# A decode step of attention and a gated MLP on one core: w_o loaded in two transfers instead of four, V's last block and w_up in plain runs, and one matmul moved

## The chip, the cores and the metric

One core of a Trainium2 chip runs the whole kernel. The time is device microseconds of one execution; a kernel's time is the median over several executions. One execution of each kernel is also recorded by the profiler. That gives the page, and behind it a trace with every instruction, every DMA packet and every semaphore event. All times inside the execution are counted from its first instruction.

## The reference

One token (x, 512 values) goes through a pre-norm attention block over a key and value cache of 65536 positions, with 32 query heads on 8 key/value heads of 128 dimensions, and then through a gated MLP of width 1792. All data are bf16.

```python
def _A_ref(x, k_cache, v_cache, wq, wo):        # x [1,1,512], wq [512,4096], wo [4096,512]
    q = (x @ wq).reshape(B, Sq, 32, 128).transpose(0, 2, 1, 3)
    k = jnp.repeat(k_cache, 4, axis=1)          # [1, 8, 65536, 128] -> 32 heads
    v = jnp.repeat(v_cache, 4, axis=1)
    scores = jnp.einsum("bhqd,bhkd->bhqk", q, k) * (128 ** -0.5)
    o = jnp.einsum("bhqk,bhkd->bhqd", _softmax(scores, axis=-1), v)
    return o.transpose(0, 2, 1, 3).reshape(B, Sq, 32 * 128) @ wo

def _B_ref(x, w_gate, w_up, w_down):            # [512,1792] twice, [1792,512]
    return (_sigmoid(x @ w_gate) * (x @ w_up)) @ w_down

h  = x + _A_ref(_layernorm(x), A_k_cache, A_v_cache, A_wq, A_wo)
h2 = h + _B_ref(_layernorm(h), B_w_gate, B_w_up, B_w_down)
```

The caches are 134 MB each. With the weights, the kernel reads 282.33 MB.

## The kernel before

**Blocks.** Each head's 65536 positions are cut into 4 blocks of 16384 (`NR` = 4), so there are 32 K blocks and 32 V blocks, K0 to K31 and V0 to V31, each of 4 MB. Partition p holds 128 consecutive positions of a block, which is one run of 32 KB in the cache. A ring of 4 slots of 32 KB per partition (`ring`) takes wq, all K and V blocks, and at the end the MLP's weights.

**Loads.** All of these loads are issued by SyncE (SP) on one queue, in the order of the list `order` (L289 to L293): wq, K0 to K3, then K and V in turns, then V28 to V31, w_gate, w_up, w_down. Each waits until its slot is free: for a K block that DVE has transposed it (`F{b}`), for a V block that PE has used it (`PV{b}`). SP issues in order, so a load that waits holds back those behind it. Directly after V28 come the loads of w_o (L347 to L352), into `ktw`, the buffer of the transposed K, when the last head's scores are done (`G7`). w_o is loaded in four pieces, `wo0` to `wo3`, of 16, 8, 4 and 4 heads (`WO`, L211). Partition p gets n consecutive rows for a piece of n heads, so the runs are 16, 8, 4 and 4 KB.

Three loads are split so that work can start on their first part. V31 (L339 to L343) is split at 3/4 into `V31.0` and `V31.1`. The block is seen as two halves of 16 KB per partition, and each transfer takes its share of both halves: two runs of 12 KB, then two of 4 KB. w_up is split into three of its four row groups and the fourth (`W_SPLIT`, L314), and w_down into 7, 5 and 2 of its 14 (`WD_SPLIT`, L212).

**Heads.** For each K block DVE transposes 8 chunks into `ktw` (L500), and PE makes the scores (L419, `ktw`). After 4 blocks there is a maximum over the head, the exponentials on ACT (L544) and a transpose on DVE (L554). One head later PE multiplies by V (L419, `ring,PT_sb`; 32 matmuls a block, four steps of 8), while the next head's K comes in. A step of V takes its rows from the first half of the block and the same place of the second half (`pv_regs`, L570; a step forward adds `CH`, L707); the K chunks are in the matching order (L495). PE's program is a loop; the parts that run only sometimes stand behind it and are branched to (`away`, L658). `head_out` (L587) normalizes a head's output and puts it into `O2`, 4 columns of 128 rows for the 4 query heads.

**The last heads.** w_o's rows are spread as n consecutive rows per partition, while `O2` holds a head's 128 dimensions on 128 partitions. `regroup(i)` (L601) brings the outputs of a piece into w_o's layout: DVE spreads the n columns over 128 columns with a mask (`blk_of`, L604), one matmul against a 0/1 matrix (`row_of`, L608) regroups them, and DVE copies the result to `O3` (L610). `project7` (L621) does this for the first three pieces, which hold the 28 heads 0 to 27, and then adds up 28 rows on PE (L627, L637, L645) into the row `yr`, to which DVE adds x (L647). It stands on PE between the work on V28 and on V29 (L763). SP issues `V31.0` when PE is done with V29, whose slot it takes. Before V31's work PE turns `yr` into columns (L649, `columns`); this part is branched to.

**The tail.** After V31: `head_out` for the last head, `regroup(3)` for its 4 query heads, 16 matmuls (L617), layer norm (L381 to L396), 16 matmuls with w_gate and 16 with w_up (L797). Between these stands the residual matmul (L803), which puts h into the PSUM bank of the final sum; it has to be there before w_down's matmuls add to that bank. Then tanh on ACT, the product (L809), a transpose (L812), 56 matmuls with w_down (L817), which wait for each of its three pieces, a copy and the output. Everything here depends on the step before.

**Setup.** DVE makes constants while wq is loaded, among them `row_of` and `blk_of` for n = 16, 8 and 4 (L369 to L373).

Of the kernel before, what the change touches and what calls it, by code (L numbers as in the profile page):

```python
# [6 lines left out]
bf16 = mybir.dt.bfloat16  # L7
fp32 = mybir.dt.float32
i32 = mybir.dt.int32
AF = mybir.ActivationFunctionType  # L10
ALU = mybir.AluOpType
# [184 lines left out]
def bass_sequential_preLN__gqa_block_cached__glu_gated_glu__decode_kernel(  # L196
# [11 lines left out]
    CH = TC * DH  # L208
    NF = FF // 128

    WO = ((0, 16), (16, 8), (24, 4), (28, 4))  # L211
    WD_SPLIT = [(0, 7), (7, 12), (12, 14)]  # L212
    FG = FF // 4

    with ExitStack() as es:
        def sb(name, shape, dt):
            return es.enter_context(nc.sbuf_tensor(name, shape, dt))
# [46 lines left out]

        W0 = NKT * CH
        O3 = sb("O3", [128, NQ], bf16)
        Lw = [sb(f"Lw{i}", [128, 128], bf16) for i in range(len(WO))]
        row_of = {n: sb(f"row_of{n}", [128, n], bf16) for n in (16, 8, 4)}
        blk_of = {n: sb(f"blk_of{n}", [128, 128 // n], bf16) for n in (16, 8, 4)}
        head_of = sb("head_of", [128, 4], fp32)  # L270
        assert 32 * D <= NKT * CH + WH
        KTW_ROW = NKT * CH + WH
# [3 lines left out]
        def ps(bank, c0, c1, p0=0, p1=128):  # L276
            return PS[p0:p1, bank * 512 + c0: bank * 512 + c1]
# [33 lines left out]

        dma("act", lambda e: e.dma_start(x_row[:, :], A_x[0]), "x", name="x")
        V_SPLIT = [(0, 3), (3, 4)]
        W_SPLIT = {"wg": [(0, 4)], "wu": [(0, 3), (3, 4)]}  # L314
        W_AT = {"wg": 0, "wu": 4 * FF}
        for ld in order:
            k, b = ld
            s = slot_of[ld]
            dst = slot_ap(s)
            deps = [freed(prev[ld])]  # L320
            if k == "wq":
                dma("sp", lambda e, d=dst: e.dma_start(d.rearrange("p (k n) -> p k n", k=4),
                    A_wq.rearrange("(p k) n -> p k n", p=128)), f"r{s}", deps, "wq")
            elif k in ("wg", "wu"):
                w = B_w_gate if k == "wg" else B_w_up
                dst, src = dst[:, W_AT[k]:W_AT[k] + 4 * FF], w.rearrange("(p k) n -> p (k n)", p=128)
                for i, (k0, k1) in enumerate(W_SPLIT[k]):
                    dma("sp", lambda e, d=dst, w=src, a=k0 * FF, z=k1 * FF: e.dma_start(d[:, a:z], w[:, a:z]),
                        f"{k}{i}", deps if i == 0 else (), f"{k}.{i}")
            elif k == "wd":  # L330
                src = B_w_down.rearrange("(p r) n -> p r n", p=128)
                for i, (r0, r1) in enumerate(WD_SPLIT):
                    dma("sp", lambda e, d2=dst[:, r0 * D:r1 * D].rearrange("p (r n) -> p r n", n=D), sr=src[:, r0:r1, :]:
                        e.dma_start(d2, sr), f"wd{i}", deps if i == 0 else (), f"wd{i}")
            else:
                h, r = b // NR, b % NR
                cache = A_k_cache if k == "K" else A_v_cache
                src = cache[0, h, r * BLK:(r + 1) * BLK, :].rearrange("(p t) d -> p (t d)", t=T)
                if ld == ("V", NB - 1):  # L339
                    for i, (c0, c1) in enumerate(V_SPLIT):  # L340
                        d2, s2 = (ap.rearrange("p (h c) -> p h c", h=2)[:, :, c0 * CH:c1 * CH] for ap in (dst, src))
                        dma("sp", lambda e, d2=d2, s2=s2: e.dma_start(d2, s2),
                            "v0" if i else "vl", deps if i == 0 else (), f"V{b}.{i}")  # L343
                else:
                    dma("sp", lambda e, d=dst, sr=src: e.dma_start(d, sr), f"v{s}" if k == "V" else f"k{s}" if k == "K" and b >= NR else f"r{s}",
                        deps, f"{k}{b}")
            if ld == ("V", NB - 4):  # L347
                for i, (j0, nj) in enumerate(WO):
                    src = A_wo[j0 * DH:(j0 + nj) * DH, :].rearrange("(p r) n -> p (r n)", r=nj)
                    dst = ktw[:, j0 * D:(j0 + nj) * D]  # L350
                    dma("sp", lambda e, src=src, dst=dst: e.dma_start(dst, src), f"wo{i}",
                        [f"G{HKV - 1}"] if i == 0 else (), f"wo{i}")  # L352
# [3 lines left out]
        for nm, t, v in (("onesf", onesf[:, :], 1.0), ("xz0", xz[:, :], 0.0), ("onef", one_f[:, :], 1.0), ("nhalf", nhalf[:, :], -0.5),  # L356
# [9 lines left out]
           (), "head")  # L366
        op("dve", lambda e: e.tensor_copy(lsel[:, :].rearrange("p (u a c) -> p u a c", a=4, c=2),
                                          bass.AP(tensor=head_of, offset=0, ap=[[4, 128], [0, 16], [1, 4], [0, 2]])), ["head"], "lsel")
        for n in (16, 8, 4):  # L369
            op("dve", lambda e, n=n: e.tensor_reduce(row_of[n][:, :], identf[:, :].rearrange("p (c r) -> p r c", r=n), AX.X, ALU.max),  # L370
               (), f"row{n}")
            op("dve", lambda e, n=n: e.tensor_reduce(blk_of[n][:, :], identf[:, :].rearrange("p (c r) -> p c r", r=n), AX.X, ALU.max),
               (), f"blk{n}")  # L373
        op("dve", lambda e: e.tensor_reduce(bass.AP(tensor=gsel, offset=0, ap=[[128, 128], [32, 4]]),
                                            identf[:, :].rearrange("p (s j) -> p s j", s=4), AX.X, ALU.add), ["gs0", "identf"], "gsel")

# [60 lines left out]
        def reg(e, i):  # L437
            while len(regs) <= i:
                regs.append(e.alloc_register(f"a{len(regs)}"))
            return regs[i]  # L440
# [18 lines left out]
                    e.reg_alu(reg(e, 4 + kt), reg(e, 4 + kt), 1024, ALU.add)  # L459
            return none(False, True)  # L460

        op("pe", project_q, ["xz", "wq", "identf", "lsel", "onef", "sel", "gsel", "row4", "PTz", "qz0"], "q")
        op("act", lambda e: e.activation(  # L463
            bass.AP(tensor=qh, offset=0, ap=[[512, 8], [64, 8], [32, 2], [1, 32]]), psap(1, 0, [[64, 8], [1, 2], [2, 32]], 0, 8), AF.Copy),
           ["q", "qh0"], "qh")
# [25 lines left out]
        def dve_block(b):  # L491
            s = slot_of[("K", b)]
            for c in range(NC):
                n = b * NC + c
                src = ring[:, s * SLOT + c * CH: s * SLOT + (c + 1) * CH].bitcast(fp32)  # L495
                dst = ktw[:, (n % NKT) * CH:(n % NKT + 1) * CH].bitcast(fp32)
                deps = [f"K{b}"] if c == 0 else []
                if b % NR or b == 0:
                    deps.append(f"S{b - 1}.{c}" if b else None)
                op("dve", lambda e, d=dst, sr=src: e.transpose(d, sr), deps, f"T{b}.{c}", to="T")  # L500
            op("dve", lambda e: e.memset(scr[:, b:b + 1], 0.0), (), f"F{b}")
            if b % NR == NR - 1:
                for k in range(NR):
                    u = b - NR + 1 + k
                    op("dve", lambda e, u=u: e.tensor_reduce(M_sb[:, u % 4:u % 4 + 1], ps(u % NS, 0, 512), AX.X, ALU.max),  # L505
                       [f"S{b}.{NC - NR + k}"], f"mx{u}", to="D")
                op("dve", lambda e: e.memset(scr[:, 32 + b // NR:33 + b // NR], 0.0), (), f"G{b // NR}")
# [56 lines left out]
        def pv_regs(e):  # L564
            for half in range(NC // NR):
                for tq in range(4):
                    i = 8 * half + tq
                    if i:
                        e.reg_alu(reg(e, i), R["p"], 2 * (128 * tq + half), ALU.add)
                        e.reg_alu(reg(e, i + 4), R["v"], 2 * (half * NR * TC + 4 * tq) * 128, ALU.add)  # L570

        def pv(b):
            h, r = b // NR, b % NR
# [22 lines left out]
            if h + 1 < HKV:  # L596
                clear_out(h + 1)

        YT, STB, GB, UB, YB, OT = 0, MISC, 2, 3, 5, (1, 2, 3, 1)

        def regroup(i):  # L601

            j0, n = WO[i]
            op("dve", lambda e: e.tensor_tensor(Lw[i][:, :].rearrange("p (j c) -> p j c", j=n),  # L604
                                                bass.AP(tensor=O2, offset=j0, ap=[[NQ, 128], [1, n], [0, 128 // n]]),
                                                bass.AP(tensor=blk_of[n], offset=0, ap=[[128 // n, 128], [0, n], [1, 128 // n]]), ALU.mult),
               [f"o2.{(j0 + n) // GS - 1}", f"blk{n}"], f"Lw{i}")
            op("pe", lambda e: e.matmul(ps(OT[i], 0, n), lhsT=Lw[i][:, :], rhs=row_of[n][:, :], start=True, stop=True),  # L608
               [f"Lw{i}", f"PT{NB - 1}" if i == 0 else None], f"O3p{i}")
            op("dve", lambda e: e.tensor_copy(O3[:, j0:j0 + n], ps(OT[i], 0, n)), [f"O3p{i}"], f"O3.{i}")  # L610

        def project(rows, src, deps, last=False):
# [6 lines left out]
                       deps if i == 0 and nt == 0 else (), "yT" if end else None)  # L619

        def project7():  # L621
            for i in range(3):
                regroup(i)
            waits = [d for i in range(3) for d in (f"O3.{i}", f"wo{i}")]
            def rows(e):
                out = ps(YB, 0, D, 0, 1)
                e.matmul(out, lhsT=O3[:, 0:1], rhs=ktw[:, 0:D], start=True, stop=False, skip_group_check=True)  # L627
# [27 lines left out]
        def pe_flow(e, section):  # L655
# [48 lines left out]
            pv_regs(e)  # L704
            section("B")
            e.reg_alu(p, p, 2 * 512, ALU.add)
            e.reg_alu(v, v, 2 * CH, ALU.add)  # L707
            e.reg_alu(m, m, -1, ALU.add)
            e.br_ne(m, 0, on_true="sums", on_false="sums_end")
            label("sums_end")  # L710
# [65 lines left out]
            if i < HKV:  # L776
                transposed(i)
        P.part = {}
        regroup(3)
        project(range(NQ - GS, NQ), O3, ["O3.3", "wo3"], last=True)  # L780


        ln_stats(1, ("yT", (YT, 0, 4)), STB, 0)
# [8 lines left out]
        for i, (nm, bank) in enumerate((("wg", GB), ("wu", UB))):  # L792
            at = slot_of[(nm, 0)] * SLOT + W_AT[nm]
            for kt in range(4):
                for c in range(4):
# [3 lines left out]
                        rhs=ring[:, at + kt * FF + c * FG: at + kt * FF + (c + 1) * FG],  # L799
                        start=(kt == 0), stop=(kt == 3), tile_position=(0, 32 * c)),  # L800
                       ["hc"] * (kt == 0 and c == 0) + dep, f"gu{i}" if kt == 3 and c == 3 else None)
            if i == 0:
                op("pe", lambda e: e.matmul(ps(YB, 0, 128), lhsT=gsel[:, :], rhs=hz[:, :], start=True, stop=False, skip_group_check=True),  # L803
                   ["hz"])

        op("act", lambda e: e.activation(sg[:, :], ps(GB, 0, FG), AF.Tanh, scale=rstd[1][:, 0:1]), ["gu0", "rstd.1"], "sg")
        op("dve", lambda e: e.tensor_scalar(sg2[:, :], sg[:, :], 1.0, rstd[1][:, 0:1], op0=ALU.add, op1=ALU.mult), ["sg"], "sg2")
# [48 lines left out]
```

## Time and profile before

| what | value |
|---|---|
| median of 4 runs | 663.4 us (662.43 to 664.38) |
| profiled execution | 662.45 us, span 660.6 us, mean granted clock 0.784 |
| busy: PE, DVE, ACT | 64%, 53%, 6% of the span |
| DMA | 282.34 MB in 11211 packets, mean 427 GB/s |
| packets under 512 B, under 8 KB | 1225, 2250 |
| K and V blocks, 4 MB each | 29.5 and 27.4 us from issue to landing |
| regrouping 28 heads (L604 to L610) | first matmul at 616.41, rows (L627) from 618.37 us |
| V31 issued, first w_gate matmul, end of w_down's | 629.10, 651.57, 658.19 us |
| output issued | 658.55 us |

The span is the time from the first to the last instruction of the profiled execution; the execution's own time is 1.85 us longer. A landing is the last of a transfer's 16 semaphore events in the trace. A transfer's time to landing is mostly time in the queue behind other transfers. In a chain of waits each line has a start, a duration and what ran; "issue" stands for time in which an engine waited for nothing that the profile shows. The clock is given as a share of full speed.

### The profile page before, as it was taken

What the parts mean: (1) busy time and instruction counts of PE and PEld (TensorE: products, weight loads), DVE (VectorE), ACT (ScalarE), POOL (GpSimd) and SP (SyncE); (2) the same over time, 40 slices, a digit from 0 to 9 for tenths busy, and PEclk for the clock granted to TensorE, in tenths of its full rate; (3) what the DMA queues carried; (4) which work ended last, traced back from release to release, by engine and by line L of the source; (5) the groups of instructions that cost most, each with busy time, mean ns of one, the idle gap of its engine ahead of it and who ended that gap; (6) DMA issues with size and microseconds to landing.
All of it is one profiled execution on the core that took longest, in us unless ns stands there. A gap on an engine that the chain in (4) does not pass through costs nothing. (4 is left out here: it accounts for less than half of the span.)

```text
span 660.6 us, 6130 instructions
## 1 busy us (share of the span) xinstructions
PE 423.7 (64%) x2316; PEld 72.9 (11%) x1548; DVE 350.5 (53%) x446; ACT 41.8 (6%) x111; POOL 3.6 (1%) x17
## 2 busy tenths in 40 slices
PE   2796587548566585666765485764856668565845
PEld 1110011011000010010100110001100001001222
DVE  3598755548437655346555374465743565553102
ACT  0100200020000200020000200002000110002000
POOL 1000000000000000000000000000000000000000
PEclk9899687678888697886966778766878758678676
DMA  9999999999999999999999999999999999999997
GB/s 381 438 419 444 425 433 440 417 444 427 431 440 417 444 429 429 440 419 442 431 427 440 419 442 431 427 440 419 442 431 427 442 419 440 431 427 423 435 422 325
DMA packets 11211, 282.34 MB, mean 427 GB/s; under 512 B 1225, under 2 KB 1226, under 8 KB 2250
## 3 DMA queue, kind: packets, MB, share of 16 engines
q1 hardware_dynamic: 11208, 282.33, 99.5%
q14 instruction: 1, 0.01, 0.0%
q10 hardware_dynamic: 2, 0.00, 0.0%
HBM read 282.33 MB, written 0.00 MB: 427 GB/s over the span
## 5 line engine op out<-in xcount | busy, mean ns | idle before, releaser
L419 PE MATMUL PS<-ktw 128*128 128x512 bf16 x1024 | 304.9, 448 | 159.6 <-DVE ktw L500 155.8
L500 DVE STREAM_TRANSPOSE ktw<-ring 128x1024 f32<-128x1024 f32 x256 | 291.8, 1206 | 136.9 <-DMA ring<-in_A_k_cache_dram 136.7
L419 PE MATMUL PS<-ring,PT_sb 128*32 x1024 | 83.3, 455 | 24.4 <-issue 16.3
L419 PEld LDWEIGHTS PS<-ktw 128*128 x256 | 27.3, 107 | 415.1 <-issue 262.3
L554 DVE STREAM_TRANSPOSE PT_sb<-P_sb 128x512 bf16<-128x512 bf16 x32 | 20.2, 684 | 53.8 <-PE PS L591 52.3
L540 ACT ACTIVATE negmax<-PS 128x1 f32<-128x1 f32 x8 | 1.4, 171 | 527.1 <-PE PS L538 527.1
L419 PEld LDWEIGHTS PS<-ring,PT_sb 128*32 x1024 | 25.4, 116 | 81.3 <-issue 76.7
L505 DVE TENSOR_REDUCE M_sb<-PS 128x1 f32<-128x512 f32 x32 | 19.9, 683 | 25.5 <-PE PS L419 25.5
L544 ACT ACTIVATE P_sb<-PS,negmax 128x512 bf16<-128x512 f32 x32 | 21.6, 686 | 0.3
L561 DVE TENSOR_REDUCE lsum<-PS 128x1 f32<-128x4 f32 x8 | 1.3, 162 | 29.3 <-PE PS L559 29.3
L531 PE MATMUL PS<-identf,gm 128*1 128x128 f32 x16 | 3.0, 271 | 16.9 <-DVE gm L529 16.9
L604 DVE TENSOR_TENSOR Lw<-O,blk_of 128x128 bf16<-128x128 bf16 x4 | 1.1, 281 | 21.8 <-ACT O L595 21.8
L588 ACT ACTIVATE po_sb<-PS,rl 128x512 bf16<-128x512 f32 x8 | 5.5, 687 | 54.9 <-PE PS L419 54.9
L466 DVE STREAM_TRANSPOSE qt<-qh 32x512 bf16<-32x512 bf16 x1 | 0.7, 699 | 15.2 <-ACT qh L463 15.2
L419 PE MATMUL PS<-ring,xz 128*8 x32 | 8.7, 439 | 0.0
L538 PE MATMUL PS<-one_f,gmrep 1*128 1x1 f32 x16 | 3.8, 303 | 5.0 <-DVE gmrep L535 5.0
L419 PE MATMUL PS<-ktw,O 128*1 x26 | 6.9, 430 | 0.0
L544 ACT ACTIVATION_READ_ACCUMULATOR P_sb<-PS,negmax 128x1 f32 x32 | 6.5, 203 | 0.0
L591 PE MATMUL PS<-sel_bf,po_sb 128*128 128x4 bf16 x32 | 2.1, 169 | 6.4 <-ACT po_sb L588 6.4
L445 PE MATMUL PS<-qz 128*8 128x512 bf16 x2 | 1.0, 481 | 6.9 <-issue 6.9
L481 ACT ACTIVATE PS<-zcol 128x512 f32<-128x512 bf16 x8 | 5.0, 622 | 0.0
L647 DVE TENSOR_TENSOR yr<-PS,x_row 1x512 f32<-1x512 f32 x1 | 0.7, 679 | 7.8 <-PE PS L645 7.8
(81 smaller groups left out, 68.6 us busy)
## 6 DMA issues: line engine op xcount, KB each, us to landing
ring<-in_A_k_cache_dram SPq DMA_DIRECT2D x32, 4096.0 KB, 29.5
ring<-in_A_v_cache_dram SPq DMA_DIRECT2D x31, 4096.0 KB, 27.4
ring<-in_A_wq_dram SPq DMA_DIRECT2D x1, 4096.0 KB, 12.3
ring<-in_A_v_cache_dram SPq DMA_DIRECT2D x1, 3072.0 KB, 13.2
ktw<-in_A_wo_dram SPq DMA_DIRECT2D x1, 2048.0 KB, 9.8
ring<-in_B_w_gate_dram SPq DMA_DIRECT2D x1, 1792.0 KB, 18.6
ring<-in_B_w_up_dram SPq DMA_DIRECT2D x1, 1344.0 KB, 21.2
ktw<-in_A_wo_dram SPq DMA_DIRECT2D x1, 1024.0 KB, 12.0
```

The source lines that it names most:

```text
L419: return e.add_instruction(mybir.InstMatmult(name=nc.get_next_instruction_name(), engine=mybir.EngineType.PE, ins=[rhs, lhsT], outs=[e.low ...
L481: op("act", lambda e: e.activation(ps(PO, 0, 512), bass.AP(tensor=zcol, offset=0, ap=[[1, 128], [0, 512]]), AF.Copy), ["zcol"] if h == 0 e ...
L500: op("dve", lambda e, d=dst, sr=src: e.transpose(d, sr), deps, f"T{b}.{c}", to="T")
L505: op("dve", lambda e, u=u: e.tensor_reduce(M_sb[:, u % 4:u % 4 + 1], ps(u % NS, 0, 512), AX.X, ALU.max), [f"S{b}.{NC - NR + k}"], f"mx{u}" ...
L531: op("pe", lambda e: e.matmul(ps(MISC, 0, 128, 0, 1), lhsT=gm[:, :], rhs=identf[:, :], start=True, stop=True), [f"gm{h}"], f"gmT{h}", to="Q")
L538: op("pe", lambda e: e.matmul(ps(MISC, 128, 129), lhsT=gmrep[0:1, :], rhs=one_f[0:1, 0:1], start=True, stop=True), [f"gmrep{h}"], f"neg{h}")
L540: op("act", lambda e: e.activation(negmax[:, k:k + 1], ps(MISC, 128, 129), AF.Copy, scale=-att_scale), [f"neg{h}"], f"negmax{h}")
L544: op("act", lambda e, b=b: e.activation(P_sb[:, (b % 4) * 512:(b % 4 + 1) * 512], ps(b % NS, 0, 512), AF.Exp, bias=negmax[:, k:k + 1], sca ...
L554: op("dve", lambda e, b=b: e.transpose(PT_sb[:, (b % 4) * 512:(b % 4 + 1) * 512], P_sb[:, (b % 4) * 512:(b % 4 + 1) * 512]), [f"E{b}", f"o ...
L561: op("dve", lambda e: e.tensor_reduce(lsum[:, :], ps(MISC, 132, 136), AX.X, ALU.add), [f"l{h}"], f"ls{h}", to="D")
L588: op("act", lambda e: e.activation(po_sb[:, :], ps(PO, 0, 512), AF.Copy, scale=rl[:, :]), [f"PV{NR * h + NR - 1}", f"rl{h}"], f"po{h}", to ...
L591: op("pe", lambda e, t=t: e.matmul(ps(OX, 0, 4), lhsT=po_sb[:, t * 128:(t + 1) * 128], rhs=sel_bf[:, 8 * t:8 * t + 8:2], start=(t == 0), s ...
```

## The change

* **w_o** comes in two transfers, of 28 heads and of 4 (`WO`). Partition p gets 28 consecutive rows, a run of 28 KB.
* **Regrouping** of the 28 heads is one DVE product of 128 x 896, seven matmuls with 128 x 4 results, and one copy. Each matmul takes every seventh column of the product as its weights. `row_of` and `blk_of` are needed for n = 4 only, so four reductions of the setup go. For the last 4 heads the shapes are those of before.
* **V31** is split at the same 3/4, but in plain runs of 24 and 8 KB per partition. A step of PE takes two neighbouring chunks in place of one from each half, for all blocks: the register constants and the order in which DVE reads the chunks of K change accordingly.
* **w_up** is one transfer, and its first matmul waits for it.
* **w_down** is cut into 9, 4 and 1 of 14 row groups.
* **The residual matmul** stands behind w_up's matmuls.

```diff
-    WO = ((0, 16), (16, 8), (24, 4), (28, 4))
-    WD_SPLIT = [(0, 7), (7, 12), (12, 14)]
+    WO = ((0, 28), (28, 4))
+    RW = 4
+    WD_SPLIT = [(0, 9), (9, 13), (13, 14)]
...
-        Lw = [sb(f"Lw{i}", [128, 128], bf16) for i in range(len(WO))]
+        Lw = [sb(f"Lw{i}", [128, n * DH // RW], bf16) for i, (_, n) in enumerate(WO)]
...
-        W_SPLIT = {"wg": [(0, 4)], "wu": [(0, 3), (3, 4)]}
+        W_SPLIT = {"wg": [(0, 4)], "wu": [(0, 4)]}
...
-                        d2, s2 = (ap.rearrange("p (h c) -> p h c", h=2)[:, :, c0 * CH:c1 * CH] for ap in (dst, src))
+                        d2, s2 = (ap[:, 2 * c0 * CH:2 * c1 * CH] for ap in (dst, src))
...
-        for n in (16, 8, 4):
-            op("dve", lambda e, n=n: e.tensor_reduce(row_of[n][:, :], ...), (), f"row{n}")
-            op("dve", lambda e, n=n: e.tensor_reduce(blk_of[n][:, :], ...), (), f"blk{n}")
+        op("dve", lambda e: e.tensor_reduce(row_of[:, :], ...), (), "row")
+        op("dve", lambda e: e.tensor_reduce(blk_of[:, :], ...), (), "blk")
...
-                src = ring[:, s * SLOT + c * CH: s * SLOT + (c + 1) * CH].bitcast(fp32)
+                at = s * SLOT + (2 * (c % NR) + c // NR) * CH
+                src = ring[:, at:at + CH].bitcast(fp32)
...
-                        e.reg_alu(reg(e, i + 4), R["v"], 2 * (half * NR * TC + 4 * tq) * 128, ALU.add)
+                        e.reg_alu(reg(e, i + 4), R["v"], 2 * (half * TC + 4 * tq) * 128, ALU.add)
...
         def regroup(i):
             j0, n = WO[i]
+            m = 128 // RW
             op("dve", lambda e: e.tensor_tensor(Lw[i][:, :].rearrange("p (j c) -> p j c", j=n),
-                                                bass.AP(tensor=O2, offset=j0, ap=[[NQ, 128], [1, n], [0, 128 // n]]),
-                                                bass.AP(tensor=blk_of[n], offset=0, ap=[[128 // n, 128], [0, n], [1, 128 // n]]), ALU.mult),
-               [f"o2.{(j0 + n) // GS - 1}", f"blk{n}"], f"Lw{i}")
-            op("pe", lambda e: e.matmul(ps(OT[i], 0, n), lhsT=Lw[i][:, :], rhs=row_of[n][:, :], start=True, stop=True),
-               [f"Lw{i}", f"PT{NB - 1}" if i == 0 else None], f"O3p{i}")
+                                                bass.AP(tensor=O2, offset=j0, ap=[[NQ, 128], [1, n], [0, m]]),
+                                                bass.AP(tensor=blk_of, offset=0, ap=[[m, 128], [0, n], [1, m]]), ALU.mult),
+               [f"o2.{(j0 + n) // GS - 1}", "blk"], f"Lw{i}")
+            for v in range(n // RW):
+                lhsT = bass.AP(tensor=Lw[i], offset=v, ap=[[n * m, 128], [n // RW, 128]])
+                op("pe", lambda e, v=v, lhsT=lhsT: e.matmul(ps(OT[i], RW * v, RW * v + RW), lhsT=lhsT, rhs=row_of[:, :], start=True,
+                                                            stop=True, skip_group_check=True),
+                   [f"Lw{i}", f"PT{NB - 1}" if i == 0 else None] if v == 0 else (), f"O3p{i}" if v == n // RW - 1 else None)
             op("dve", lambda e: e.tensor_copy(O3[:, j0:j0 + n], ps(OT[i], 0, n)), [f"O3p{i}"], f"O3.{i}")
...
         def project7():
-            for i in range(3):
-                regroup(i)
-            waits = [d for i in range(3) for d in (f"O3.{i}", f"wo{i}")]
+            regroup(0)
+            waits = ["O3.0", "wo0"]
...
-            e.reg_alu(v, v, 2 * CH, ALU.add)
+            e.reg_alu(v, v, 2 * 2 * CH, ALU.add)
...
-            if i == 0:
-                op("pe", lambda e: e.matmul(ps(YB, 0, 128), lhsT=gsel[:, :], rhs=hz[:, :], start=True, stop=False, skip_group_check=True),
-                   ["hz"])
+        op("pe", lambda e: e.matmul(ps(YB, 0, 128), lhsT=gsel[:, :], rhs=hz[:, :], start=True, stop=False, skip_group_check=True), ["hz"])
```

## The prediction

> **What bounds the kernel now.** I read the busy slices and the DMA queue of the page first, then the landings, then the chain of waits, last the tail in windows of 50 ns.
>
> ```profile
> DMA  9999999999999999999999999999999999999997
> ...
> q1 hardware_dynamic: 11208, 282.33, 99.5%
> ```
>
> One queue carries 282.33 MB and is busy 99.5% of the 660.6 us span; no slice but the last is below 9. Its landings are as even: in the trace's landing records (the last of a transfer's 16 semaphore events) the 4 MB blocks follow each other every 9.71 us (9.703 to 9.726) from 22.69 us to 605.49. PE (64%), DVE (53%) and ACT (6%) work beside it. So an edit counts if it shortens this stream, or the work after its last landing. The last landings:
>
> ```
> wo0 610.40  wo1 612.90  wo2 614.18  wo3 615.45  V29 625.16  V30 634.86
> V31.0 642.25  V31.1 644.81  wg 649.10  wu.0 652.35  wu.1 653.47
> wd0 655.66  wd1 657.24  wd2 657.86
> ```
>
> The chain of waits runs beside it and ends at the same moment:
>
> ```profile
> 635.46 3.19 PE PS L419 x31
> 638.64 2.09 issue
> 640.73 2.02 PE PS L653 x8
> 642.75 0.13 issue
> 642.88 2.76 PE PS L419 x24
> ...
> 651.57 1.66 PE PS L797 x16
> 653.23 0.73 PE PS L803 x2
> 653.96 1.49 PE PS L797 x14
> 655.45 0.02 issue
> 655.47 0.92 DVE hh L809
> 656.39 0.02 issue
> 656.41 0.66 DVE hhT L812
> 657.07 0.04 issue
> 657.12 1.09 PE PS L817 x56
> ```
>
> The reader is to see that L803, the residual matmul, stands between the two halves of L797 (gate and up), and that PE is never free from 635.46 on but for the 2.09 us at 638.64, which have no wait behind them. The chain names PE alone for the last 1.09 us; the windows of L817 show what it hides:
>
> ```profile
> 657.75:657.80 0.05, 0.05 (x16) 0.02 (x4) 1.00 0.00 0
> 657.80:657.85 0.05, 0.05 (x12) 0.00 (x0) 1.00 0.00 0
> 657.85:657.90 0.05, 0.05 (x9) 0.00 (x1) 1.00 0.00 0
> 657.90:657.95 0.05, 0.05 (x8) 0.05 (x8) 1.00 0.00 0
> ```
>
> The columns after the time are PE busy and then PEld, weight loads. The loads stop at 657.77 and go on at 657.90, for the last 8 matmuls: that is wd2, landed at 657.855. So the last transfer sets the end, by 0.13 us against the chain. From its landing to PE's last end are 0.335 us (658.19), then the copy and the output's 2.4 us, which the change leaves alone.
>
> **The change, part by part.** *The stream.* Bytes stay. What a cut into more transfers or shorter runs costs stands in the landings, for three places. Calling the 128 packets of one run per partition a group: wo in four groups takes 9.952 us against 9.712 for a plain block (0.240 for 3 groups more); V31 in four groups (two transfers of two runs) 9.947 (0.235 for 3); w_up in two 3.251 + 1.119 = 4.370 against 4.289 of w_gate in one (0.081 for 1). So a group costs 0.08 us. The change takes away two of wo, two of V31, one of w_up: 5 x 0.08 = **0.40 us**. w_down keeps three groups, only cut elsewhere: 0. The bounds: below, only w_up's 0.08, if nothing but the transfer that is shown in both forms behaves so; above, the packet records (32768 B take 1217 ns, 16384 B 614.5, so 11.7 ns are fixed): 640 packets fewer over 16 engines, 0.47, and 0.03 for three transfers' closing packets of 9 ns, 0.50. I take 0.40, as three places agree. wd2 then lands at 657.46.
>
> The trace shows three added transfers costing 0.24 us together while the queue is full. The Trainium skill ("DMA: Bandwidth & Descriptors", section on the anatomy of one DMA, gpsimd path) gives a fixed cost of about 2.0 us per DMA; three fewer would by it bring an estimated 6 us. These transfers go through SP's queue back to back, and the rows decide against that sum.
>
> *The tail behind the last transfer.* wd2 holds 4 matmuls in place of 8. Loads are issued 13.5 ns apart (48 from 657.12 to 657.77), so 4 fewer give 0.05 us. End of PE: 657.46 + 0.335 - 0.05 = 657.74 against 658.19: **0.45 us**.
>
> *Whether the chain keeps up.* It starts at V30's landing, 0.16 earlier by wo's two groups. V31.0 (642.00) and V31.1 (644.49) land before PE comes for them (642.59 and 645.5), so the 0.16 stays up to w_gate's end, 653.07 (653.23 less 0.16). There L803 stood; its 0.73 us now lie behind w_up, beside hh and hhT (1.58 us together), which cover it; without that cover it would cost its 0.73 again. The new wait: the first up matmul waits for w_up whole, 653.47 - 0.40 = 653.07, plus 0.05 as wd2's wake shows. Behind it in PE's queue stand L803 and the down matmuls, and DVE's hh waits for gu1. So up starts at 653.12, takes 1.52 (the timeline: 653.89 to 655.41), and hhT is done 1.66 later (655.41 to 657.07), at 656.30. The down matmuls begin at 656.35, before 657.12. wd0 has 9 rows now; it lands near 655.86 (seven rows took 2.188, 0.301 each with 0.08 for the group), 0.49 before it is wanted: covered. 36 matmuls at 13.5 ns end at 656.8; wd1 lands some 0.37 before wd2, near 657.09. So PE is 0.3 us ahead of the stream, and what is late next is the stream itself. If w_up lands without any saving (653.47), the chain is 0.40 later and PE still arrives before wd2.
>
> *Regrouping.* Before, three rounds of DVE, PE, DVE fill 616.41 to 618.37. Now one product of 128x896 and seven matmuls with weights of stride 14 bytes, which the trace does not show. The product: 0.9 us by L807 (448 elements in 0.45) to 1.8 by L809 (448 in 0.91); it starts at 612.43, where Lw0 starts, and PE comes at 616.2: free. The matmuls: 0.30 us by L617 (16 in 0.69, stride 8 bytes) to 2.1 by L608 alone (load 0.10 plus 0.20, seven times); I take 0.4, L617 being the strided one. With copy and hand-over rows start 0.75 to 2.55 us after 616.41, against 1.96: between 1.2 us sooner and 0.6 later. Queued behind are the rows (to 625.9), PV29, and through it SP's issue of V31:
>
> ```profile
> 629.10 1.31 SPq L342 DMA_DIRECT2D ring<-in_A_v_cache_dram  x2
> ```
>
> V30 is still on its way until 634.86, so the queue has 5.7 us of cover here, and PE waits 6.39 us for V30. Only beyond 5.7 us does this reach the end. The single wo of 28 heads lands at 605.49 + 8.5 = 614.0, wo2 before at 614.18; PE comes at 616.2. Not late. The last regroup (four heads) keeps its shape: 128x128, one matmul.
>
> *Setup and registers.* Four DVE reductions go: 3.34 to 4.29 us, 0.95 us. PE waits for wq until 13.05 and xz is done at 7.88: hidden by 5.2 us, no gain. K's transposes read the same 8 chunks in another order, and PV adds another constant: nothing.
>
> *Sum.* 0.45 us off the profiled execution: 662.45 (span 660.6, 1.85 around it) becomes 662.0. That execution lies 0.95 under the median of the four runs, 663.4; I move the median by as much: **662.95**.
>
> **The rivals.** *A, forecast: 662.95.* *B, the gain is lost behind the last landing: 663.4.* The granted clock is 0.5 from 641.5 to 655.1 and 1.0 in the down stage. If the shifted work leaves the down matmuls at 0.5, they take an estimated 27 ns each (L797 at 0.5: 1.52 / 16 for 448 columns, scaled to 128): 56 from 656.35 end at 657.86, and 0.3 of drain gives 658.16: nothing gained. Against it: the busy windows before 655.14 stay busy in the new order. The same 663.4 follows if groups do not cost what I read from them.
>
> *C, slower: PE's idle time without a wait.* The 2.09 us at 638.64 come when PE goes to a part of its program that is branched to (columns, section VZ); 1.96 at 604.09 is its like, before a loop branched back to. The change adds four matmuls to the block written out before that one and so moves all branch targets behind it. One more such idle time between 635 and 656 shifts the chain by 2.09: down matmuls from 658.44, PE's end 0.94 later (657.12 to 658.19 less the gap of 0.13) at 659.38, so 1.19 above before: **664.6**. It makes the kernel slower from a delay of 0.90 on (656.35 + 0.90 + 0.94 = 658.19), and by over 0.2% from 2.23 on, so one stall and a little, or two. For it: the 2.09 are on the chain already, in a block of this kind. Against it: 18 idle times of the kind sum to 16.3 us, mostly in the loop that the change does not lengthen; and the stall could as well shrink, which brings nothing. The Trainium skill ("Runtime: NRT & Kernel Launch", section on instruction fetch) has a taken branch out of the window stop for a fetch; it gives no price, and speaks for C only if a target crosses such a bound.
>
> *D, the strided regroup is dear.* Above 0.8 us a matmul the 5.7 us of cover are gone. No row of a bf16 weight load is above 0.155 us. At twice that bound, 1.6 each, the queue stands still for 5.5 us: 668.5.
>
> **How the numbers follow.** A 0.63, B 0.20, C 0.15, D 0.02. The four runs spread from 662.43 to 664.38, 1 us to each side, so a measurement of this kernel tells some 0.2% (1.33 us) from no change. A's gain is a third of that; with the runs' spread added, 0.15 of A and B end faster by over 0.2%, 0.05 slower by over 0.2%, and 0.63 within. C, one stall or more, splits at 2.23 us: 0.08 slower by over 0.2%, 0.07 within. D is slower. Faster 0.15, same 0.70, slower 0.15. Range: below, A's largest gain (0.50 + 0.05) and 1.0 of spread, 661.8; above, one stall of C, 664.6, which leaves out C's longer ones, D and some of the spread.
>
> **What the profile after would show.** Packets 11211 - 5 x 128 - 3 x 16 = 10523; those under 512 B 1177. wo and V31 land in 9.79 us each in place of 9.95, w_up in 4.29, and wd2 0.40 us earlier against the first K block. L803 behind both halves of L797, hh 0.8 us earlier, and a gap in L817 before its last four. Right only if the 2.09 us at 638.64 stay what they are. Wrong if the landings keep their 9.95, if a second idle time without releaser stands in the tail, or if the clock in the down stage is 0.5.

## The result and the profile after

| | before | after |
|---|---|---|
| median | 663.18 us (60 runs, 662.43 to 664.77) | 665.39 us (38 runs, 662.48 to 666.68) |
| ratio after / before | | 1.0022, 95% interval 1.0014 to 1.0030 |
| profiled execution, span | 662.45, 660.6 us | 662.88, 660.8 us |

The kernel became slower, by 0.22% over all compared runs (the medians, between two groups, differ by more); forecast were 662.95 us and no measurable change. The median hides that the runs after the change form two groups. The table splits each run's time into its span and the time outside the span (the run's time less its own span), over all 40 recorded runs:

```
                  runs   span, median   outside the span
before             117      661.0       1.76 to 3.44, median 1.96
after, group 1      19      660.7       2.05 to 2.16
after, group 2      20      661.0       5.10 to 5.68
after, one run       1      661.2       3.66
```

(The 117 are runs of the kernel before beside four groups of experiments; one of 677 us is left out.) Inside the span nothing got worse. The loss lies outside it, in half of the runs: their median is 5.36 us there, 3.3 above group 1 and 3.4 above the kernel before. The profiled execution belongs to group 1, so its profile shows what became of the prediction's steps. The packets and queues of the page:

```profile
DMA packets 10523, 282.35 MB, mean 427 GB/s; under 512 B 1177, under 2 KB 1306, under 8 KB 1562
...
q1 hardware_dynamic: 10520, 282.33, 99.5%
q8 instruction: 1, 0.02, 0.0%
```

The packets are the 10523 forecast. New against the page of before is the last line: one packet of 16 KB of instructions, on queue 8. (A kernel with PE's program at its old length can have it too; a table further down lists these packets.) The chain of waits now ends in the stream:

```profile
631.35 26.08 DMA ring<-in_B_w_down_dram
657.43 0.04 issue
657.47 0.56 PE PS L817 x20
658.03 0.02 issue
658.05 0.29 DVE y_sb L821
```

and the tail by instructions (start, duration, what; in brackets the idle time before it and what ended it):

```profile
653.39 1.64 PE L799 MATMUL PS<-ring,hc 128*1 128x448 bf16 x16 [0.23 <-DMA ring<-in_B_w_up_dram]
...
654.96 0.49 PE L804 MATMUL PS<-hz,gsel 128*128 128x128 f32 x2
655.09 0.92 DVE L809 TENSOR_TENSOR hh<-PS,sg 128x448 bf16<-128x448 f32 x1 [0.75 <-PE PS L799]
656.04 0.65 DVE L812 STREAM_TRANSPOSE hhT<-hh 128x448 bf16<-128x448 bf16 x1
...
657.47 0.39 PEld L817 LDWEIGHTS PS<-ring,hhT 128*1 128x1 bf16 x20 [0.25 <-DMA ring<-in_B_w_down_dram]
```

The reader is to see that up waits for w_up, that the residual (now L804) lies beside hh, and that the down matmuls wait for their second piece: PE is ahead of the stream. From V27's landing to the last the stream took 51.98 us against 52.36:

```
          w_o     V31     w_up    w_down   V27 to last
before    9.952   9.947   4.370   4.385    52.361
after     9.785   9.795   4.295   4.383    51.982
```

The other traces agree. From V27 to the last landing takes 52.36 to 52.39 us in those with all the old cuts, 52.11 to 52.14 with three groups of 128 packets fewer (b_stream and its two variants below), and 51.96 to 51.99 with five fewer. (Two traces with an instruction packet inside the stream and one with a late V31 are left out.)

### The profile page after: what moved, and what is told of

Same layout as the page of the kernel before. It is cut to its first block, busy times and chain, and to the rows that moved or that the text cites. A ratio compares the mean times of both kernels' runs of the same rounds, so it can differ in the third digit from the quotient of the medians.

```text
span 660.8 us, 6126 instructions
## 1 busy us (share of the span) xinstructions
PE 423.9 (64%) x2320; PEld 73.3 (11%) x1552; DVE 349.6 (53%) x438; ACT 41.8 (6%) x111; POOL 3.6 (1%) x17
## 2 busy tenths in 40 slices
DMA packets 10523, 282.35 MB, mean 427 GB/s; under 512 B 1177, under 2 KB 1306, under 8 KB 1562
## 5 line engine op out<-in xcount | busy, mean ns | idle before, releaser
L604 DVE TENSOR_TENSOR Lw<-O,blk_of 128x896 bf16<-128x896 bf16 (+1 forms) x2 | 1.4, 682 | 22.5 <-ACT O L594 22.5
```

## The experiments

An engine's compiled program is a row of instruction words. Theory 1: PE's program grew from 487 to 494 words, and this costs time behind the last instruction. Rivals: SP's program, 132 to 129 words (theory 2), DVE's, 219 to 211 (theory 3), or the new w_o part itself (theory 4). "Idle words" are increments of a semaphore that nobody waits for.

**b_pe7**: the kernel before with idle words at the end of PE's program.

```diff
+            for i in range(7):
+                e.sem_inc(pad_sem, 1)
+        op("pe", pad)
```

> The kernel before with seven idle semaphore increments at the end of PE's program (487 words become 494, as many as after the change); nothing else. Theory 1 (PE's longer program costs time behind the last instruction): a second group of runs appears some 3.3 us above the first, time outside the span 2.1 or 5.3 us, median near 665; and the profile shows one instruction packet of 16 KB near 659 us. Theory 2 (SP's shorter program does it) and theory 3 (DVE's shorter program does it): one group, 662.4 to 664, as before.

Median 664.42; ratio 1.0019 (1.0007 to 1.0032). Outside: 2.1 to 5.24, median 3.27. The time outside grew as theory 1 says, but the runs scatter (two of twelve are above 5 us) instead of forming two groups. And the experiment has a flaw: each idle word took 0.15 us, so PE ended 1 us later.

**a_sp3**, **a_dve8**: the kernel after with SP's or DVE's program at its old length (for a_dve8 eight words, ahead of DVE's last copy).

```diff
+            for i in range(3):
+                e.sem_inc(pad_sem, 1)
+        op("sp", pad)
```

> The kernel after with three idle semaphore increments in SP's program ahead of the output (129 words become 132, as before). Theory 2 (SP's program length): one group near 662.4, outside the span 1.85. Theories 1 and 3: two groups as after the change, 662.5 to 663.2 and 665.9 to 666.7.

> The kernel after with eight idle semaphore increments late in DVE's program (211 words become 219, as before). Theory 3 (DVE's program length): one group near 662.4. Theories 1 and 2: two groups as after the change.

Medians 662.94 and 666.31. Both keep the second group (4 of 12 runs and 9 of 12 above 5 us): theories 2 and 3 fall. But a_sp3's span is 660.65 (median) against 660.9 of after and 661.0 of a_dve8, and the traces show a place for it. SP's last branch and its drain, the instruction that closes its program, lie 0.15 us apart in a_sp3, 0.16 in before, 0.45 in after and a_dve8. So SP's length seems to cost something inside the span; the next pair tests that.

**b_stream**, **b_stream_sp1**: the stream's edits on the kernel before, w_o and the regrouping left as they were; then with SP at 132 words. (The reading order that goes with V31's plain runs, and the residual behind up, are in both and are not printed here.)

```diff
-    WD_SPLIT = [(0, 7), (7, 12), (12, 14)]
+    WD_SPLIT = [(0, 9), (9, 13), (13, 14)]
...
-        W_SPLIT = {"wg": [(0, 4)], "wu": [(0, 3), (3, 4)]}
+        W_SPLIT = {"wg": [(0, 4)], "wu": [(0, 4)]}
...
-                        d2, s2 = (ap.rearrange("p (h c) -> p h c", h=2)[:, :, c0 * CH:c1 * CH] for ap in (dst, src))
+                        d2, s2 = (ap[:, 2 * c0 * CH:2 * c1 * CH] for ap in (dst, src))
...
+        op("sp", pad)        # b_stream_sp1 alone: one idle word
```

> The kernel before with the edits of the stream that leave PE's program at 487 words: V31 in plain runs, w_up whole, w_down cut 9, 4, 1, and the residual matmul behind w_up; w_o and the regrouping stay. SP's program is one word shorter. Theory 1: one group, three groups of packets fewer (0.24 us) and 4 matmuls fewer behind the last landing (0.05): 0.2 to 0.3 us under before, near 662.9. Theory 2: a second group may appear. Theory 3: one group.

> The edits of the stream alone on the kernel before (V31 in plain runs, w_up whole, w_down cut 9, 4, 1, residual behind w_up), now with SP's program padded from 131 to 132 words. If SP's shorter program costs the 0.3 us between SP's last branch and its drain: that step takes 0.15 in place of 0.44, the span falls by 0.3 to 660.7, and the median to 662.5. If SP's length does not matter: as without the pad, span 661.0, median 662.8.

662.78 and 662.65 (ratios 0.9995 and 0.9993, the latter 0.9984 to 1.0002); spans 661.0 and 660.7; branch to drain 0.44 and 0.15. One word of SP makes this difference. One group each. Over all fifteen experiments the step is 0.15 to 0.16 with 132 words of SP and 0.44 to 0.45 with 129 or 131.

**a_x_sp3**, **a_x**: the kernel after with PE at 485 words, since x is loaded as columns instead of being turned by four matmuls; SP at 132 or 129.

```diff
+        dma("act", lambda e: e.dma_start(x_col[:, :], A_x[0].rearrange("o (p k) -> (o p) k", k=4)), "xc", name="xc")
...
-        for kt in range(4):
-            lhsT = bass.AP(tensor=x_row, offset=kt, ap=[[D, 1], [4, 128]])
-            op("pe", lambda e, lhsT=lhsT, kt=kt: e.matmul(ps(MISC, kt, kt + 1), lhsT=lhsT, rhs=ident[0:1, 0:1], start=True, stop=True,
-                                                          skip_group_check=True),
-               ["x", "ident"] if kt == 0 else (), "xTp" if kt == 3 else None)
```

> The kernel after with PE's program cut from 494 to 485 words (x comes as columns by a second small DMA on ACT's queue, in place of four matmuls of the setup, which the wait for wq covers) and SP's program padded from 129 to 132 words. Theory 1 (length of PE's program): one group of runs, outside the span 1.8 to 2.1, and with the stream's 0.40 and SP's 0.3 kept a span near 660.6 and a median near 662.5, 0.5 under before. Theory 4 (the regrouping itself, or anything else of w_o's part, makes the second group): two groups, 662.3 and 665.9, as with SP padded alone.

> The kernel after with PE's program cut to 485 words by loading x as columns, and SP's left at 129 words. Theory 1: one group outside the span. SP's length adds its 0.3 us inside the span: SP's drain 0.44 us behind its branch in place of 0.15, span near 660.9 to 661.1, median near 662.9. If SP's length does not matter: as with 132 words, median 662.6.

662.67 and 662.91; outside, medians 1.85 and 1.84, none above 3.5; spans 660.8 and 661.1. The w_o part is in both, so the new regrouping is not the cause: theory 4 falls.

**b_pe3**: the kernel before with 490 words, three idle ones at PE's end, as in b_pe7.

> The kernel before with three idle words at the end of PE's program (490). Theory 1 with a sharp bound between 487 and 494 words: either all as before (one group, median 663.0) or as with seven words (median 664.4, runs up to 666). Theory 1 with a gradual effect: some runs above 664.5, fewer than with seven words.

663.33; outside 2.0 to 2.96, median 2.33. Nothing at 5 us; the median is 0.26 above that of the kernel before beside it (2.07, up to 3.06). So there is perhaps a small rise ahead of the step.

**b_pe8_head**: the kernel before with 494 words, eight idle ones at PE's head, ahead of its wait for wq.

> The kernel before with eight idle semaphore increments at the head of PE's program, while PE waits for x; the compiled program has 494 words, as after the change, and PE's end is not delayed. Theory 1 (length of PE's program): time outside the span in two groups, 2.1 and 5.2 us, as after the change. Theory 1c (what counted in the run with idle words at the end was that PE ended 1 us later): as before, 1.8 to 2.1 with a few up to 3.4.

666.16; outside 5.18 to 5.46 in all five runs, span 660.8. PE ends when it did before. This is the cleanest of the set: words that cost nothing where they stand take 3.3 us behind the end. a_x, on the same chip with 485 words, has no run above 2.6. The two groups that were expected did not appear: with 494 words 4 of 12, 9 of 12, 20 of 40 and here 5 of 5 runs lie above 5 us, and what sets that share stays open.

**a_sp3_pe40**: a_sp3 with 534 words of PE, forty idle ones at its end.

> The kernel after with SP padded to 132 words and forty idle words at the end of PE's program (534). Theory 1a (a bound that the end of PE's program must not come close to from below): with the end well beyond it the fetch falls early, one group near 662.4 to 663. Theory 1b (every longer program): two groups, 662.3 and 665.9, or all runs near 666.

668.04, span 665.4; outside 1.96 to 3.51, no run at 5 us. The forty idle words took 6 us at the end, so PE ends with the span here and the question is not answered. Two things are seen: a 16 KB instruction packet now falls at 621.96 us, inside the stream, where V29 then lands 11.13 us after w_o in place of 9.71; and a second one starts behind the span.

**b_pe30_head**: the kernel before with 516 words, thirty idle ones at PE's head.

> The kernel before with thirty idle words at the head of PE's program (516 words), while PE waits for x and wq; PE's end is not delayed. Theory 1a (a bound in PE's program that its end must not just reach): the second 16 KB instruction packet falls early, ahead of PE's end, no group at 5.2 us outside the span; if it falls into the stream it delays the landings behind it by about 1 us. Theory 1b (every longer program pays behind the end): all runs at 5.2 us outside the span or above, median 666.

664.14 (1.0013, 1.0004 to 1.0022); outside 1.84, no run above 2.65; span 661.9. So it is a bound, not every word; whether the kernel after loses its second group with more words is not tested. (The kernels with 490, 516 and 534 words ran on other chips than the padded ones with 494; the kernel before ran beside each and has no run above 3.44 outside.) The packet, in the queues between 619 and 623 us:

```profile
q1 hardware_dynamic: 52, 1.70, 99.7%
q8 instruction: 1, 0.02, 1.7%
```

It starts at 620.57 and takes 1.07 us. V29 lands 10.82 us after w_o in place of 9.71, and all later landings stay 1.1 us late: the same packet, paid in the stream.

**b_x**, **b_stream_x_sp1**: the kernel before and b_stream_sp1 with x as columns, 478 words.

> The kernel before with x loaded as columns (478 words of PE in place of 487) and nothing else. If the scatter outside the span that the kernel before itself shows (1.8 in most runs, up to 3.4 in some) is the foot of the same effect: all runs near 1.8, median 0.1 to 0.2 us under before. If not: as before.

> The edits of the stream on the kernel before, with x as columns (478 words of PE) and SP padded to 132 words; w_o and the regrouping as before. By all that the runs showed so far this is the shortest: span 660.7, outside 1.8, median 662.5, 0.5 to 0.6 us under before and under the kernel after in every one of its groups.

b_x: outside 1.77 to 1.97, as expected if the scatter of the kernel before belongs to the same effect. That is not shown, though: b_stream has 487 words and 1.78 to 1.99, a_x_sp3 has 485 and runs up to 3.5. The span is 661.3, 0.4 above the kernel before beside it, and the median 663.09. b_stream_x_sp1: 662.71 (0.9994, 0.9985 to 1.0003), no better than b_stream_sp1; its span is 660.8 against 660.7.

**a_x_rows_sp3**: a_x_sp3 cut to 482 words of PE, by adding up w_o's rows one matmul a turn.

```diff
-                e.reg_mov(left, n // 2 - 1)
+                e.reg_mov(left, n - 2)
...
-                for x, y in ((ra, ro), (rb, rp)):
-                    mm_at(e, out, at_reg(O3, y, [[NQ, 128], [1, 1]]), at_reg(ktw, x, [[KTW_ROW, 128], [1, D]]), False, 32)
+                mm_at(e, out, at_reg(O3, ro, [[NQ, 128], [1, 1]]), at_reg(ktw, ra, [[KTW_ROW, 128], [1, D]]), False, 32)
```

> The kernel after with PE's program cut to 482 words (x as columns, and the 28 rows of w_o added up one matmul a turn instead of two) and SP's padded to 132. If the time outside the span grows gradually with PE's length: 1.8 in nearly all runs, none above 2.5; median near 662.4, 0.6 under before. With a bound between 487 and 490 words: as with 485 words, a few runs up to 3.5.

663.82 (1.0013, 1.0005 to 1.0022): outside 1.85 as expected, but span 661.7. The rows take longer and SP issues V31 4 us later:

```profile
617.65 10.23 PE L414 MATMUL PS<-ktw,O 128*1 x26
...
633.11 0.80 SPq L345 DMA_DIRECT2D ring<-in_A_v_cache_dram  x2
```

V31's first transfer then lands 7.79 us behind V30, where after and a_x_sp3 have 7.31: 0.48 late. The profiled execution is the fastest of the eleven (span 661.0).

**a_x_sp3_resmid**: a_x_sp3 with the residual back between gate and up.

> The kernel after with PE at 485 words, SP at 132, and the residual matmul back between gate and up. By the prediction's chain, the residual's 0.73 us replace a wait of 0.2 us for w_up, so hhT ends 0.5 us later, the down matmuls begin near 657.2 and no longer wait for a transfer before the last: PE's end some 0.2 to 0.3 us later, span 660.9 to 661.0. If the move was free of effect because the last landing sets the end anyway: the gap ahead of the last four matmuls stays and the span is 660.7.

662.90, span 660.9 against 660.8 of a_x_sp3: not told apart by time. The chain:

```profile
652.93 0.73 PE PS L802 x2
653.66 1.62 PE PS L796 x14
...
656.25 0.66 DVE hhT L811
656.90 0.04 issue
656.95 1.69 PE PS L816 x56
```

hhT ends at 656.90 in both traces, but w_up landed at 653.37 here and at 653.53 in a_x_sp3. Behind its landing up starts 0.22 us later here, because of the residual, and 0.05 there. Against the last landing the down matmuls end 0.86 and 0.70 us behind it: the residual's place is worth some 0.16 us, too little to see in the medians. The 56 down matmuls take 1.69 us in both, without a gap. That goes with the granted clock. The microsecond from 657 to 658 in after, in a_sp3 and here, the clock in the third column from the right:

```profile
657.00:658.00 1.00, 0.94 (x52) 0.52 (x36) 0.00 (x0) 0.00 (x0) 0.00 (x0) 1.00 0.02 6
```

```profile
657.00:658.00 1.00, 1.00 (x52) 1.00 (x40) 0.00 (x0) 0.00 (x0) 0.00 (x0) 0.50 0.03 8
```

```profile
657.00:658.00 1.00, 1.00 (x44) 1.00 (x48) 0.00 (x0) 0.00 (x0) 0.00 (x0) 0.50 0.05 17
```

All counts together (without a_sp3_pe40):

```
PE words                                  runs   outside above 5 us   median outside
478 (b_x, b_stream_x_sp1)                  22            0               1.8
482, 485 (four kernels)                    45            0               1.8
487 (before; b_stream, b_stream_sp1)      139            0               1.8 to 2.0
490 (b_pe3)                                11            0               2.3
494 (five kernels)                         81           40               2.1 or 5.2
516 (b_pe30_head)                          11            0               1.8, span 0.9 longer
```

The five kernels with 494 words are after, a_sp3, a_dve8, b_pe7 (whose own median is 3.3) and b_pe8_head.

## Why the prediction was wrong

**The step that failed** is the end of the sum: "then the copy and the output's 2.4 us, which the change leaves alone", and the 1.85 us around the span, carried over as a constant. Neither stayed. From PE's last end to the end of the span it is 2.77 us in place of 2.4 (658.00 to 660.77), of which 0.3 is SP's step. And the change lengthens PE's program by 7 words (4 matmuls of 2 words, one wait less): outside the span one half of the runs has 2.1 us and the other 5.36, where the sum had 1.85. That the length does this is shown, by the idle words that bring the second group into the kernel before (b_pe8_head) and by the shorter program that takes it out of the kernel after (a_x, a_x_sp3).

How it does so is only partly seen. The packet records run on past the span. Here is every 16 KB instruction packet of the profiled executions, in us from the first instruction (the executions that are not listed show none):

```
                 PE words   16 KB packet     time outside
b_stream_x_sp1      478     659.47-660.73       1.8
b_stream            487     659.14-660.14       1.8
b_pe3               490     663.57-664.86       2.8
after               494     659.07-660.05       2.1
a_sp3               494     663.09-664.02       5.2
a_dve8              494     663.38-664.53       5.4
b_pe8_head          494     663.10-664.27       5.4
b_pe7               494     662.26-663.19       3.6
b_pe30_head         516     620.57-621.64       1.8
a_sp3_pe40          534     621.96-623.02
                            667.77-669.14       3.5
```

Where the packet comes early, while the output is under way, the run is short. Where it comes after the span, the four executions with 494 words end 1.7 to 1.9 us behind the packet's end (with the run's time counted from the first instruction), as if they had waited for it. But b_pe3 and a_sp3_pe40 end 0.2 us before theirs, so a late packet alone is not a wait; nor is the packet new with 494 words. That PE waits for the words in it with 494 and not with 490 or 534 would fit all rows; it is inferred, and no record names the waiting. Why the packet comes early in some runs and late in others stays open, as does the reason of SP's 0.3 us.

The Trainium skill ("Runtime: NRT & Kernel Launch", section on instruction fetch mechanics) has the instruction memory refilled in 16 KiB blocks of 256 instructions. The packet of 16384 B agrees; two blocks are 512 words, an estimate of where the bound lies if some eighteen words stand around the program of 494, which no run here shows. The page calls the cost of crossing from one block to the next mostly hidden. If these packets are such crossings, it was not hidden here: 3.3 us at the end, 1.1 and 1.4 in a full stream.

**Rival C** had the right suspicion, four matmuls that lengthen PE's program, and the wrong place: the idle time at columns shrank, from 2.09 to 1.69 us, and no other came into the tail. In the timeline of after:

```profile
640.81 2.02 PE L655 MATMUL PS<-one_f,yr 1*128 1x1 f32 x8 [1.69 <-issue]
```

**The stream: right.** Forecast 0.40 us, measured 0.38 (52.361 - 51.982); w_o 9.79 and 9.785, V31 9.79 and 9.795, w_up 4.29 and 4.295. The sign that was named, the last landing against the first K block, shows only 0.21 us (634.96 against 635.17): the sixty blocks between took 0.17 us more in this execution, and over all traces they vary by 0.24. **The tail behind the last landing: right**, 0.285 forecast, 0.27 measured (657.732 to 658.00). **The chain: right in its order**: up starts 0.04 behind w_up's landing, hhT is done before w_down's second piece lands. By the clock of the execution hh starts 0.38 us earlier, not 0.8, since w_up landed at 653.35 and not at 653.07. **Regrouping: right in size**: seven matmuls 0.53 (0.4 taken), the product 1.07, rows 0.8 us behind the first matmul.

**Its cover was too wide.** "5.7 us of cover" counted to V30's landing. a_x_rows_sp3 issued V31 1.95 us ahead of that landing (635.06) and lost 0.48, so the cover ends some 2.4 us earlier, at about 3.3: an estimate from this one trace.

**The gain did not arrive whole even in group 1.** Its span's median is 660.7 against 661.0, 0.3 of the 0.45. SP's shorter program takes back 0.3 between branch and drain. Group 1's median of 662.85 lies close to the forecast 662.95, but by luck: the sum started from a median of four runs that is 0.2 above that of sixty. **Rival B** is real beside it: at a clock of 0.5 the down matmuls take 1.66 us (1.51 estimated), and a_sp3 ends 0.69 us behind its last landing instead of 0.27. Which clock the stage gets changes from trace to trace: the clock's record moves in steps of 3.41 us, and the last one at 1.0 begins at 654.87 us in after and at 645.50 in a_sp3.

## What to carry to other kernels

Count the instruction words of each engine's program before and after an edit: seven words more, close to a bound, cost more here than all the edits saved. Compare time outside the span run by run when a kernel's times fall into groups; a profile of one execution shows only the group it fell into. No version was clearly faster than the kernel before: the best, b_stream_sp1, has a median 0.5 us lower, with an interval that holds 1. A stream that is full gives its price per group of 128 packets in its own landings, and the five groups' price held to 0.02 us.

## What was not expected of the hardware

* A 16 KB instruction packet goes over the same DMA engines as the data: in a full stream it made every later landing 1.1 us late (b_pe30_head), and the first and the last event of a landing moved apart from 0.53 to 1.64 us. In a_sp3_pe40 it was 1.4 us.
* An idle semaphore increment on PE took 0.15 us, so forty of them 6 us.
* With 128 packets of 8 bytes on ACT's queue at the start (x by columns) the span was 0.4 us longer in b_x and 0.1 to 0.2 in the three other pairs of kernels with and without it; that the packets are the cause is not shown.
